# A new order of instructions and a new spread over the engines for a gated linear attention with a feed-forward layer, with the same operations and transfers

## The chip, the cores and the metric

The kernel runs on one core of a Trainium2 chip. The metric is the device time of one execution in microseconds (us). Five engines run side by side, each through a list of its own: TensorE (PE, matrix multiplications into PSUM), ScalarE (ACT), VectorE (DVE), GpSimd (POOL) and SyncE (SP). They wait for each other through semaphores. GpSimd issues the transfers of the weights, SyncE all others.

## The reference

The attention part runs over 4 batches x 8 heads, 768 steps and 48 elements a head. The feed-forward part takes the 3072 tokens of 384 elements.

```python
f = 1.0 / (1.0 + np.exp(-f_logit))
for t in range(S):
    state = f[:, :, t, :, None] * state + np.einsum('bhd,bhe->bhde', k[:, :, t], v[:, :, t])
    y[:, :, t] = np.einsum('bhd,bhde->bhe', q[:, :, t], state)
x = y.transpose(0, 2, 1, 3).reshape(B * S, H * D)
out = (np.maximum(x @ w_gate, 0.0) * (x @ w_val)) @ w_out
```

w_gate and w_val are 384 x 1536, w_out is 1536 x 384. Inputs and output are float32; the matmuls run in bfloat16.

## The kernel before

**Units.** The attention is computed in 12 units of 256 steps of one batch, in the order batch 0 to 3 for the first 256 steps, then the second, then the third. A unit loads f, k, q and v (one transfer of SyncE each, into four buffers per input). ScalarE makes exp and logarithm of f (L536, L538). PE sums the logarithms along the steps (L545, L546, "cumulative sum"). ScalarE takes exponentials of the sums (L560, L567), with which VectorE or GpSimd multiply q and k (L579, L585, written to `hats`). `hats` is transposed, by PE (L634) and a copy to `qkT`, or for later units by a transposing transfer of SyncE. PE then makes scores (L669), which are masked into `ptm`: by VectorE in one step (L683), or by a copy of ScalarE (L678) and a product of GpSimd (L680). PE forms the new state from k and v (L723, L734), VectorE and GpSimd update it (L508, L512, L515). The input v is cast into `vpad` and `vrest` by four to six small copies a unit (L380, L382 and L383 are the lines of the copy helper for VectorE's reduction form, for ScalarE, and for a plain copy). Per unit there are two y groups of PE (L767, L774, L778), of 128 steps each. A y is copied to `xT`, directly or through `xn` and a transposing transfer of SyncE (L797).

**Feed-forward.** Four y make 512 tokens. For each of 12 slices j of the hidden size, PE computes a gate group and a value group (L814, three matmuls each over xT and wg or wv), ScalarE applies relu (L819), and VectorE multiplies both into `gT` (L821). The first 512 tokens are taken in two halves of 256 for j = 0 to 2. Then, for each 128 tokens, four out groups of three matmuls (L837) sum over j; the result is copied to `osb` and stored by SyncE (L858). The weights come in four pieces of three slices for each of wg, wv, wo (288 KB each); GpSimd issues them (L477). wg0 is issued only when the second k (k1) has landed, wg3 when q3 has.

**Order.** Operations are numbered as the program adds them. Which engine an operation runs on is in a table per unit, the order on each engine in `SEQUENCE`, and which of eight PSUM banks a tile lies in, and after which other tile, in `HOMES`. The list is fixed: an engine whose next operation waits does not take one behind it. Before its first matmul of an operation PE may run `FILLERS`, matmuls of zeros whose result is not used; they stand in front of the waits for data.

```python
first = 'f0 k0 v0 q0 v1 f1 q3 q1 k1 wg0@k1 wv0@k0 wg1@f0 wv1@k0 ... wg3@q3 wo0@k0 wv3@f0 ...'.split()
FILLERS = {66: 4, 84: 11, 89: 2, 232: 5, 124: 1, 127: 2, 153: 1}
```

Some numbers that are spoken of below:

| Operation | What it is |
|---|---|
| 45, 46, 47, 48, 50, 49, 51, 53 (POOL) | issues of wg0, wv0, wg1, wv1, wv2, wg2, wg3, wv3 |
| 52, 57, 55, 56 (POOL) | issues of wo0, wo1, wo2, wo3 |
| 101, 140 (POOL) | state products of units 0 and 1 (L515) |
| 109; 281, 285 (POOL) | q products of unit 1; of unit 3 (L579) |
| 130; 254, 257, 259 (POOL) | mask products of unit 1; of unit 2 (L680) |
| 116, 245 (POOL after) | casts of v |
| 120, 122, 249, 247, 294, 292 (PE) | transposes of units 1, 2 and 3 |
| 149, 153, 145; 151, 155, 147 (PE) | gate; value groups of the first 256 tokens, j = 0 to 2 |
| 134, 137 (PE) | the two y groups of unit 1 |
| 205 to 212, 217 to 224 (PE) | out groups of the first 512 tokens; 205, 206, 217, 218 use wo0, and 211 is the first to use wo3 in the list |
| 307; 308; 309 (PE; ACT; SP) | first y group of unit 3, its copy to xn, its transposing transfer |
| 142, 270, 143, 315 (SP) | loads of k for unit 4, f for unit 5, q for unit 4, f for unit 6 |
| 369, 412 (PE) | cumulative sums of units 4 and 5 |
| 390, 435; 393 (PE; ACT) | scores of units 4 and 5; ScalarE's copy of scores of unit 4 |

Of the kernel before, what the change touches and what calls it, by code (L numbers as in the profile page):

```python
# [246 lines left out]
FILLERS = {66: 4, 84: 11, 89: 2, 232: 5, 124: 1, 127: 2, 153: 1}  # L247


def bass_hgrn2_outer__then__ffn_reglu_kernel(  # L250
# [725 lines left out]
```

## Time and profile before

| What | Value |
|---|---|
| Time, median of 3 runs | 194.19 us (193.44 to 194.41) |
| Profiled execution: its own time | 193.8 us |
| Profiled execution: span from first to last instruction | 192.0 us |
| PE busy | 181.1 us (94%) |
| DVE busy | 126.3 us (66%) |
| ACT busy | 118.5 us (62%) |
| POOL busy | 82.8 us (43%) |
| Moved by DMA | 31.89 MB, mean 166 GB/s |
| Granted TensorE clock | 1.000 |

A row of the order of events gives start, length, engine, line, operation, written and read tiles, and in brackets the idle time of the engine ahead of it and what released it. That releaser is inferred. In the chain of waits a row is start, length and what the end of the span hung on.

### The profile page before, as it was taken

How to read it: one execution, taken by the hardware profiler on the slowest of the kernel's cores; microseconds unless marked ns; L12 is line 12 of the kernel's file. 1: busy time of each engine (PE TensorE's matmuls, PEld its weight loads, DVE VectorE, ACT ScalarE, POOL GpSimd, SP SyncE). 2: the span in 40 equal slices, each digit the busy share in tenths (PEclk: the TensorE clock that was granted, in tenths of full speed). 3: DMA queues.
4: the chain of work that ended last, by engine and by line, in shares of the span. 5: the costliest groups of instructions: out<-in, count | busy, mean ns of one | idle time of the engine just before them, and what ended most of it. 6: DMA issues, size and time to landing. Idle time of an engine off the chain costs nothing.

```text
span 192.0 us, 4436 instructions
## 1 busy us (share of the span) xinstructions
PE 181.1 (94%) x1746; PEld 101.0 (53%) x1770; DVE 126.3 (66%) x238; ACT 118.5 (62%) x233; POOL 82.8 (43%) x110
## 2 busy tenths in 40 slices
PE   3998799998999999999999999999999999999994
PEld 1365474545654646455655456454655554445563
DVE  4189864879499999987669989445277452242451
ACT  4998668681997877978687857247702642433511
POOL 4458553994247256754696749007500320000000
DMA  6999999999599999999974792564144050000325
GB/s 156 324 325 285 205 253 206 242 231 199 145 310 220 229 323 255 245 213 189 259 202 79 153 232 59 120 130 123 50 107 79 0 164 3 20 0 0 81 66 164
DMA packets 79088, 31.89 MB, mean 166 GB/s; under 512 B 71254, under 2 KB 79068, under 8 KB 79068
## 3 DMA queue, kind: packets, MB, share of 16 engines
q1 hardware_dynamic: 74268, 28.08, 59.7%
q0 software_dynamic: 4800, 3.54, 11.9%
q8 instruction: 14, 0.23, 0.5%
q14 instruction: 6, 0.05, 0.1%
HBM read 25.96 MB, written 4.73 MB: 160 GB/s over the span
## 4 chain that ended last, share of the span: by engine, by line
PE 75%; DMA 6%; DVE 6%; ACT 4%; SPq 3%; issue 3%; POOL 2%; POOLq 0%
PE ps L814 43%; PE ps L837 22%; DMA wv<-in_moe_w_val_dram 4%; SPq L449 3%; DMA v_in<-in_v_dram 3%; PE ps L669 2%; PE ps L767 2%; DVE gT L821 2%; DVE ptm L683 1%; PE ps L634 1%; ACT ptm L678 1%; ACT relu L819 1%; PE ps L545 1%; DVE vpad L380 1%; POOL vpad L383 1%
## 5 line engine op out<-in xcount | busy, mean ns | idle before, releaser
L821 DVE TENSOR_TENSOR gT<-relu,ps 128x512 bf16<-128x512 bf16 (+1 forms) x75 | 47.7, 660 | 32.9 <-PE ps L814 19.6
L819 ACT ACTIVATE relu<-ps 128x512 bf16<-128x512 f32 (+1 forms) x75 | 41.8, 582 | 37.1 <-PE ps L814 29.1
L837 PE MATMUL ps<-wo,gT 128*128 128x384 bf16 (+2 forms) x300 | 56.2, 320 | 0.9 <-DVE vrest L380 0.8
L814 PE MATMUL ps<-xT,wv 128*128 128x512 bf16 (+1 forms) x214 | 54.6, 370 | 1.3 <-DMA wv<-in_moe_w_val_dram 0.4
L814 PE MATMUL ps<-xT,wg 128*128 128x512 bf16 (+1 forms) x214 | 54.2, 370 | 1.2 <-DMA wg<-in_moe_w_gate_dram 0.5
L680 POOL TENSOR_TENSOR ptm<-ptm,seen 128x512 bf16<-128x512 bf16 x21 | 24.0, 1155 | 39.9 <-ACT ptm L678 39.8
L837 PEld LDWEIGHTS ps<-wo,gT 128*128 128x128 bf16 x300 | 28.0, 98 | 22.4 <-DVE vrest L380 1.2
L814 PEld LDWEIGHTS ps<-xT,wg 128*128 128x128 bf16 x225 | 21.1, 98 | 21.3 <-DMA wg<-in_moe_w_gate_dram 0.8
L814 PEld LDWEIGHTS ps<-xT,wv 128*128 128x128 bf16 x225 | 20.9, 98 | 20.5 <-DVE hats L579 0.6
L683 DVE TENSOR_TENSOR ptm<-ps,seen 128x512 bf16<-128x512 f32 x27 | 18.1, 685 | 1.9 <-PE ps L669 1.7
L585 DVE TENSOR_TENSOR hats<-k_in,ps 64x384 bf16<-64x384 f32 x28 | 15.4, 550 | 5.2 <-ACT ps L567 4.7
L515 POOL TENSOR_TENSOR st<-ssum,dec 128x384 bf16<-128x384 f32 x16 | 13.3, 832 | 11.0 <-DVE ssum L512 10.1
L585 POOL TENSOR_TENSOR hats<-q_in,expo 64x384 bf16<-64x384 f32 x16 | 15.9, 995 | 4.8 <-ACT expo L560 3.8
L678 ACT ACTIVATE ptm<-ps 128x512 bf16<-128x512 f32 x21 | 11.8, 595 | 8.5 <-PE ps L669 8.5
L579 POOL TENSOR_TENSOR hats<-q_in,expo 128x384 bf16<-128x384 f32 x11 | 10.9, 999 | 12.8 <-ACT expo L560 8.2
L382 ACT ACTIVATE osb<-ps 128x384 f32<-128x384 f32 x13 | 6.5, 499 | 12.0 <-PE ps L837 12.0
L560 ACT ACTIVATE expo<-ps 128x384 f32<-128x384 f32 x20 | 9.4, 492 | 3.4 <-DVE ps L549 2.8
L512 DVE TENSOR_TENSOR ssum<-ps,st 128x384 f32<-128x384 f32 x16 | 8.8, 553 | 3.7 <-PE ps L723 2.3
L536 ACT ACTIVATE f_in<-f_in 128x768 f32<-128x768 f32 x12 | 10.2, 847 | 1.1 <-DMA f_in<-in_f_logit_dram 1.0
L567 ACT ACTIVATE ps<-ps 128x384 f32<-128x384 f32 x22 | 10.6, 497 | 0.0
L538 ACT ACTIVATE bneg<-f_in 128x768 bf16<-128x768 f32 x12 | 10.2, 848 | 0.2
L383 DVE COPY osb<-ps 128x384 f32<-128x384 f32 (+2 forms) x12 | 6.2, 520 | 5.5 <-PE ps L837 5.5
(86 smaller groups left out, 185.1 us busy)
## 6 DMA issues: line engine op xcount, KB each, us to landing
f_in<-in_f_logit_dram SPq DMA_DIRECT2D x12, 384.0 KB, 5.8
v_in<-in_v_dram SPq DMA_DIRECT2D x12, 384.0 KB, 5.3
q_in<-in_q_dram SPq DMA_DIRECT2D x12, 384.0 KB, 4.9
k_in<-in_k_dram SPq DMA_DIRECT2D x12, 384.0 KB, 5.4
out_dram<-osb SPq DMA_DIRECT2D x15, 192.0 KB, 2.1
out_dram<-osb SPq DMA_DIRECT2D x16, 96.0 KB, 2.2
wg<-in_moe_w_gate_dram POOLq DMA_DIRECT2D x4, 288.0 KB, 8.4
wv<-in_moe_w_val_dram POOLq DMA_DIRECT2D x4, 288.0 KB, 8.1
```

What stands on the lines that cost most here:

```text
L515: add(e, lambda: engine[e].tensor_tensor(t4(s_new), t4(tmp), rate, ALU.mult), [key] + dk, [f"S{b}_{y}"], **(dict(occ=0.79, lat=0.1) if e = ...
L536: add("ACT", lambda cut=cut: sc.activation(raw["f"][:, cut], raw["f"][:, cut], AF.Exp, scale=-1.0), [f"f{li}"], [f"f{li}"], **act_t(2 * HD ...
L567: add("ACT", lambda i=i, ex=ex: sc.activation(bc[i].ap[:, 0:HD] if in_place else ex[:, 1, :], bc[i].ap[:, 0:HD], AF.Exp, scale=1.0), [bc[i ...
L579: add(e, lambda i=i, n=n, x=x, e=e, exps=exps: engine[e].tensor_tensor(hats[:, hi, i, x, :, 0:D], by_i[n][:, i, :, :], exps(), ALU.mult), ...
L585: op = add(e, lambda i=i, n=n, x=x, e=e, y=y, lo=lo, exps=exps: engine[e].tensor_tensor(hats[64 * i:64 * i + 64, hi, y, x, :, 0:D], by_i[n ...
L678: add("ACT", lambda pt=pt, s=sj[j]: sc.activation(pt, s.ap[:, :].rearrange("p (n t) -> p n t", n=NP), AF.Copy), [sj[j]], [f"raw{mis[y]}_{j ...
L680: add("POOL", lambda pt=pt, mask=mask: gp.tensor_tensor(pt, pt, mask, ALU.mult), [f"raw{mis[y]}_{j}", "seen"], [f"raw{mis[y]}_{j}", f"ptm{ ...
L683: add("DVE", lambda pt=pt, mask=mask, s=sj[j]: ve.tensor_tensor(pt, s.ap[:, :].rearrange("p (n t) -> p n t", n=NP), mask, ALU.mult), [sj[j ...
L814: mm = te.matmul(bank.ap[:, 0:n], wt[:, kt, j * 128:(j + 1) * 128], xT[xi][:, kt, n0:n1], start=(kt == 0), stop=(kt == NK - 1))
L819: add("ACT", lambda: sc.activation(relu[ri][:, 0:n], gate.ap[:, 0:n], AF.Relu), [gate], [f"relu{ri}"], **act_t(n))
L821: add("DVE", lambda: ve.tensor_tensor(gT[gi][:, j, n0:n1], relu[ri][:, 0:n], val.ap[:, 0:n], ALU.mult), [val, f"relu{ri}"], [f"gT{gi}_{j}_ ...
L837: mm = te.matmul(bank.ap[:, 0:cut[1] - cut[0]], gT[gi][:, j, r * C:(r + 1) * C], wo[:, j, cut[0]:cut[1]], start=(j == 0), stop=(j == NJ - 1))
```

## The change

The set of operations, their sizes and the transfers are the same. Their numbers stay. Changed are the lists of all five engines, the banks, the fillers (31 in place of 26), and for some copies, casts and multiplies the engine:

| Group | before | after |
|---|---|---|
| casts of v to vpad and vrest | ACT 21, DVE 23, POOL 14 | ACT 14, DVE 17, POOL 27 |
| copies of y to xT or xn | ACT 18, DVE 6 | ACT 10, DVE 14 |
| copies of the output to osb | ACT 13, DVE 12 | ACT 10, DVE 15 |
| copies of PE's transposes to qkT | ACT 4, DVE 6 | ACT 5, DVE 5 |
| q multiplies | DVE 5, POOL 27 | DVE 6, POOL 26 |

The beginning of three of the lists, and the fillers:

```diff
     "PE": [
-        1040, 66, 67, 84, 92, 131, 104, 82, 105, 89, 94, 232, 260, 86, 98, 231, 120, 122, 133, 95, 124, 127, 153, 249, 145, 149, 151, 134, 137, 147,
-        247, 155, 157, 159, 161, 173, 167, 165, 163, 175, 251, 255, 177, 276, 169, 171, 179, 189, 187, 181, 183, 294, 185, 191, 292, 201, 203, 197,
-        296, 299, 193, 205, 199, 195, 206, 262, 207, 304, 208, 210, 209, 211, 307, 306, 218, 220, 263, 311, 266, 217, 369, 212, 219, 221, 395, 222,
-        223, 224, 321, 323, 319, 412, 337, 397, 325, 331, 327, 339, 329, 335, 341, 439, 333, 351, 345, 343, 428, 347, 430, 556, 387, 441, 353, 349,
-        435, 390, 355, 529, 359, 432, 361, 530, 357, 398, 442, 402, 446, 363, 574, 365, 472, 573, 458, 456, 474, 454, 464, 459, 470, 482, 460, 490,
...
+        1040, 66, 67, 84, 92, 82, 105, 94, 104, 131, 89, 98, 86, 231, 232, 120, 122, 260, 95, 124, 127, 249, 133, 149, 153, 145, 134, 137, 151, 155,
+        247, 165, 159, 157, 161, 147, 167, 175, 255, 251, 171, 304, 179, 169, 276, 173, 163, 177, 191, 185, 181, 189, 294, 187, 292, 193, 201, 183,
+        197, 296, 299, 199, 203, 195, 307, 218, 206, 217, 205, 207, 219, 306, 262, 209, 208, 369, 211, 221, 210, 311, 263, 266, 220, 222, 319, 327,
+        321, 223, 323, 335, 212, 412, 224, 331, 325, 333, 339, 337, 329, 395, 397, 347, 341, 343, 345, 351, 556, 439, 428, 430, 387, 441, 390, 353,
+        432, 435, 529, 359, 355, 349, 573, 363, 361, 357, 530, 442, 398, 446, 402, 365, 458, 574, 459, 460, 482, 461, 454, 490, 468, 456, 472, 464,
...
     "POOL": [
-        33, 3, 8, 9, 20, 32, 6, 31, 0, 4, 1, 7, 30, 71, 35, 21, 75, 80, 117, 115, 119, 45, 109, 46, 47, 34, 48, 130, 50, 49, 51, 53, 52, 259, 285,
-        281, 57, 101, 55, 254, 56, 257, 140, 241, 242, 289, 303, 301, 269, 382, 380, 375, 401, 417, 314, 421, 427, 541, 445, 392, 394, 438, 449, 585,
...
+        33, 20, 0, 1, 3, 4, 8, 31, 9, 32, 30, 21, 80, 6, 7, 71, 119, 117, 45, 109, 46, 48, 101, 116, 47, 130, 50, 49, 51, 35, 34, 140, 53, 257, 281,
+        285, 254, 52, 57, 259, 55, 245, 56, 287, 291, 241, 242, 301, 243, 303, 380, 383, 375, 269, 427, 314, 384, 421, 417, 423, 401, 425, 424, 426,
...
     "SP": [
-        36, 38, 39, 41, 37, 58, 40, 43, 44, 54, 60, 59, 42, 61, 62, 63, 141, 270, 142, 144, 315, 309, 143, 273, 318, 271, 272, 406, 450, 386, 385,
...
+        36, 38, 39, 41, 37, 40, 43, 58, 44, 54, 60, 59, 42, 61, 62, 63, 141, 144, 309, 142, 270, 143, 315, 273, 271, 406, 272, 450, 385, 318, 386,
...
-FILLERS = {66: 4, 84: 11, 89: 2, 232: 5, 124: 1, 127: 2, 153: 1}
+FILLERS = {66: 10, 84: 9, 82: 1, 98: 8, 124: 2, 149: 1}
```

More of the change, by code (lines that the diff above doesn't have):

```diff
@@ L240 @@
-    [
-        13, 60, 29, 67, 75, 49, 50, 83, 87, 118, 123, 125, 133, 166, 107, 110, 137, 173, 170, 152, 158, 224, 192, 218, 197, 222, 204, 265, 238, 268,
-        241, 249, 255, 278, 282, 287, 292, 303, 299, 309],
-    [
-        2, 61, 64, 40, 76, 77, 82, 51, 85, 112, 120, 99, 126, 117, 165, 136, 142, 168, 183, 180, 153, 160, 221, 187, 219, 194, 227, 231, 206, 210,
-        270, 237, 275, 276, 252, 279, 283, 290, 300, 304],
+        312, 10, 61, 29, 37, 39, 44, 80, 86, 71, 112, 95, 101, 114, 127, 177, 143, 142, 148, 180, 159, 163, 189, 194, 201, 232, 266, 212, 268, 239,
@@ new lines @@
+        243, 269, 274, 255, 260, 302, 304],
+    [
+        0, 21, 16, 19, 26, 64, 34, 83, 42, 48, 50, 51, 72, 87, 88, 90, 124, 93, 172, 115, 108, 167, 136, 139, 168, 181, 215, 196, 197, 200, 231, 267,
+        214, 235, 272, 245, 259, 278, 279, 280, 291, 300, 285, 310],
+    [
+        1, 13, 62, 20, 30, 27, 67, 43, 79, 57, 98, 102, 126, 128, 103, 165, 137, 173, 170, 184, 153, 160, 190, 217, 222, 208, 209, 207, 211, 270, 237,
+        247, 254, 277, 258, 295, 292, 297, 307],
+    [
+        3, 6, 4, 11, 65, 24, 36, 69, 40, 49, 81, 58, 94, 99, 132, 129, 134, 111, 141, 144, 171, 183, 179, 216, 225, 191, 218, 193, 195, 227, 203, 265,
+        234, 236, 256, 287, 293, 305, 299],
@@ new lines @@
+    [
+        8, 12, 15, 18, 28, 32, 41, 78, 52, 56, 73, 92, 119, 131, 117, 130, 106, 109, 138, 145, 147, 151, 175, 185, 186, 156, 188, 192, 219, 199, 229,
+        205, 263, 242, 273, 248, 257, 283, 286, 284, 294, 301],
+    [
+        2, 7, 60, 31, 76, 77, 82, 59, 118, 104, 133, 107, 122, 146, 169, 149, 182, 157, 154, 187, 261, 226, 223, 210, 240, 249, 276, 288, 296, 306,
+        308],
+    [
+        14, 63, 17, 22, 25, 33, 66, 38, 35, 46, 54, 53, 85, 74, 89, 96, 91, 97, 100, 125, 105, 166, 110, 121, 178, 174, 140, 152, 158, 162, 161, 221,
+        230, 220, 204, 198, 213, 238, 233, 241, 244, 246, 281, 303, 298, 311],
@@ L246 @@
+    [
+        9, 5, 70, 23, 68, 75, 47, 45, 55, 84, 113, 123, 120, 116, 164, 135, 150, 176, 155, 224, 262, 228, 206, 202, 264, 271, 250, 251, 275, 252, 253,
+        282, 289, 290, 309],
 ]
-FILLERS = {66: 4, 84: 11, 89: 2, 232: 5, 124: 1, 127: 2, 153: 1}
+FILLERS = {66: 10, 84: 9, 82: 1, 98: 8, 124: 2, 149: 1}
 def bass_hgrn2_outer__then__ffn_reglu_kernel(
@@ L781, in out_of @@
         x_key = [f"xT{xi}_{r}"]
-        wait = [] if y or not {0: {'kps': False, 'qps': False, 'q0': 'POOL', 'q1': 'POOL', 'even': 'PE', 'm00': 'DVE', 'm01': 'DVE', 'm10': 'DVE', 'tk': 'DVE', 'm11': 'DVE', 'r1': 'POOL', 'tq': 'ACT', 'v11': 'ACT', 'v10': 'DVE', 'r0': 'ACT', 'v01': 'ACT', 'v00': 'DVE1', 'vb': 'DVE1', 'pr': False, 'o1': 'DVE', 'vc0': 'DVE', 'x0': 'ACT', 'x1': 'ACT', 'yy': True, 'o0': 'ACT', 'vc1': 'ACT'}, 1: {'kps': True, 'r0': 'ACT', 'm01': 'DVE', 'm00': 'DVE', 'tq': 'DVE', 'v11': 'POOL', 'even': 'PE', 'tk': 'ACT', 'q1': 'DVE', 'v00': 'DVE1', 'm11': 'POOL', 'r1': 'DVE', 'm10': 'DVE', 'v01': 'POOL', 'v10': 'POOL', 'q0': 'POOL', 'qps': False, 'yy': False, 'td': False, 'vb': 'DVE', 'vc0': 'DVE', 'o0': 'DVE', 'vc1': 'DVE', 'x0': 'ACT', 'o1': 'ACT'}, 2: {'tk': 'DVE', 'v01': 'POOL', 'kps': True, 'r1': 'ACT', 'r0': 'ACT', 'even': 'PE', 'q0': 'DVE', 'v00': 'POOL', 'v10': 'ACT', 'm00': 'DVE', 'v11': 'DVE1', 'm01': 'POOL', 'm11': 'POOL', 'tq': 'DVE', 'q1': 'POOL', 'm10': 'POOL', 'qps': True, 'x0': 'ACT', 'vc1': 'ACT', 'pr': False, 'vc0': 'DVE', 'o0': 'DVE', 'x1': 'ACT', 'vb': 'POOL'}, 4: {'v10': 'DVE1', 'v01': 'POOL', 'm00': 'DVE', 'q11': 'POOL', 'q00': 'POOL', 'q01': 'POOL', 'q0': 'POOL', 'kps': True, 'even': 'DVE', 'm01': 'DVE', 'v00': 'ACT', 'm10': 'POOL', 'q10': 'POOL', 'q1': 'POOL', 'm11': 'POOL', 'v11': 'DVE1', 'qps': False, 'tq': 'DVE', 'r0': 'ACT', 'tk': 'DVE', 'r1': 'ACT', 'yy': True, 'o1': 'ACT', 'o0': 'DVE', 'x1': 'DVE', 'x0': 'DVE'}, 10: {'m00': 'POOL', 'm10': 'POOL', 'q0': 'POOL', 'kps': True, 'q10': 'POOL', 'm01': 'POOL', 'q11': 'POOL', 'q00': 'POOL', 'v11': 'ACT', 'even': 'DVE', 'v01': 'DVE1', 'v00': 'POOL', 'q01': 'POOL', 'q1': 'POOL', 'm11': 'DVE', 'v10': 'ACT', 'td': True, 'o0': 'DVE'}, 9: {'v11': 'ACT', 'v10': 'ACT', 'even': 'DVE', 'kps': True, 'q1': 'POOL', 'm10': 'DVE', 'v00': 'ACT', 'm11': 'POOL', 'q11': 'POOL', 'm00': 'DVE', 'q00': 'POOL', 'q10': 'POOL', 'q0': 'POOL', 'q01': 'POOL', 'v01': 'DVE1', 'm01': 'DVE', 'yy': False, 'x0': 'DVE', 'td': True, 'o0': 'DVE'}, 3: {'kps': True, 'm00': 'DVE', 'm11': 'POOL', 'v11': 'DVE1', 'm10': 'POOL', 'tk': 'ACT', 'v01': 'DVE1', 'r1': 'DVE1', 'tq': 'DVE', 'q1': 'POOL', 'v00': 'DVE1', 'v10': 'POOL', 'q0': 'POOL', 'r0': 'DVE1', 'm01': 'DVE', 'even': 'DVE', 'qps': False, 'vb': 'DVE1', 'x1': 'ACT', 'o1': 'DVE', 'vc1': 'ACT', 'pr': False, 'vc0': 'DVE', 'o0': 'ACT'}, 5: {'q1': 'POOL', 'm00': 'DVE', 'kps': True, 'q11': 'POOL', 'v10': 'ACT', 'v00': 'DVE1', 'even': 'DVE', 'q01': 'POOL', 'm11': 'POOL', 'q00': 'POOL', 'q0': 'POOL', 'v11': 'POOL', 'm01': 'DVE', 'q10': 'POOL', 'v01': 'ACT', 'm10': 'DVE', 'tq': 'ACT', 'r0': 'DVE1', 'tk': 'DVE', 'r1': 'DVE1', 'qps': False, 'o1': 'ACT', 'x0': 'DVE', 'o0': 'ACT', 'yy': False}, 11: {'q0': 'POOL', 'v01': 'ACT', 'q10': 'POOL', 'm00': 'DVE', 'q01': 'POOL', 'm11': 'POOL', 'q1': 'POOL', 'q00': 'POOL', 'kps': True, 'v11': 'ACT', 'm01': 'DVE', 'q11': 'POOL', 'even': 'DVE', 'v00': 'DVE1', 'm10': 'POOL', 'v10': 'DVE1', 'yy': True, 'o1': 'DVE', 'td': True}, 7: {'v10': 'POOL', 'kps': True, 'q1': 'POOL', 'v01': 'POOL', 'q11': 'POOL', 'm00': 'DVE', 'v11': 'DVE1', 'even': 'PE', 'm10': 'POOL', 'm11': 'DVE', 'm01': 'POOL', 'q10': 'POOL', 'qps': False, 'q01': 'POOL', 'q0': 'POOL', 'o0': 'DVE', 'x1': 'DVE', 'td': True, 'x0': 'ACT', 'o1': 'ACT'}, 8: {'m10': 'DVE', 'v11': 'ACT', 'q01': 'POOL', 'm01': 'POOL', 'even': 'DVE', 'q0': 'POOL', 'v10': 'ACT', 'q1': 'POOL', 'm00': 'DVE', 'kps': True, 'q11': 'POOL', 'q00': 'POOL', 'qps': False, 'v00': 'DVE1', 'q10': 'POOL', 'v01': 'ACT', 'pr': False, 'td': True, 'x0': 'DVE'}, 6: {'v10': 'DVE1', 'v01': 'DVE1', 'q10': 'DVE', 'm10': 'DVE', 'kps': True, 'q1': 'DVE', 'even': 'PE', 'q01': 'POOL', 'm00': 'POOL', 'm01': 'POOL', 'q11': 'DVE', 'q00': 'DVE', 'm11': 'POOL', 'qps': True, 'q0': 'DVE', 'pr': False, 'o0': 'DVE', 'yy': False, 'o1': 'DVE'}}.get(u, {}).get("yy") else [f"{n}{(2 * u + 1) % NM}_{j}" for j in range(2) for n in ("raw", "ptm")]
```

27 lines of the change are left out of this document (8 added, 19 removed), and 63 rows, old and new, of the table SEQUENCE.

## The prediction

> **What bounds the kernel now.** I read the page's busy shares and slices first, then busy time by stage, then the chain of waits in order of time, and last the order of events on TensorE, GpSimd, VectorE and SyncE around the few places where TensorE stands still.
>
> ```profile
> span 192.0 us, 4436 instructions
> PE 181.1 (94%) x1746; PEld 101.0 (53%) x1770; DVE 126.3 (66%) x238; ACT 118.5 (62%) x233; POOL 82.8 (43%) x110
> PE   3998799998999999999999999999999999999994
> DMA  6999999999599999999974792564144050000325
> ```
> ```profile
> 0.00:24.00 24.00, 18.02 (x232) 9.98 (x238) 16.21 (x44) 18.35 (x35) 13.63 (x34) 1.00 1.09 259
> 24.00:40.00 16.00, 15.90 (x169) 9.58 (x171) 10.06 (x21) 11.59 (x23) 10.58 (x13) 1.00 1.24 234
> 40.00:48.00 8.00, 7.00 (x81) 4.07 (x81) 7.32 (x13) 3.67 (x9) 5.06 (x8) 1.00 1.07 211
> 48.00:184.00 136.00, 134.55 (x1230) 73.48 (x1248) 90.79 (x158) 83.91 (x165) 53.49 (x58) 1.00 0.59 142
> 184.00:192.00 8.00, 5.63 (x47) 3.90 (x45) 1.96 (x5) 0.98 (x2) 0.00 (x0) 1.00 0.41 112
> ```
> TensorE is busy for 181.1 of 192.0 us. The second fence gives, per stretch, its length, then busy time of PE, PEld, DVE, ACT and POOL. From 48 to 184 us PE idles 136.00 - 134.55 = 1.45 us in all: no order of the same instructions can take more than that out of 71% of the span. PE is free for 6.0 us before 24 us (and runs fillers there besides), 1.0 us from 40 to 48, and at the tail, whose last store the change leaves last. So the change acts in the first 48 us, where the DMA slices stand at 9: weights and loads set the pace.
>
> ```profile
> 14.27 0.90 POOL wg L477
> ...
> 15.24 0.95 POOL hats L579
> 16.19 7.17 DMA wv<-in_moe_w_val_dram
> ...
> 23.49 0.49 PE ps L814 x3
> 23.98 0.73 PE ps L767 x44
> ...
> 29.17 0.55 PE ps L669 x16
> ...
> 35.34 0.45 PE ps L634 x8
> ...
> 40.77 0.49 PE ps L837 x3
> 41.26 0.66 PE ps L814 x3
> ```
> ```profile
> 14.24 0.93 POOL L477 DMA_DIRECT2D wg<-in_moe_w_gate_dram  x1 [1.07 <-DMA k_in<-in_k_dram]
> ...
> 21.45 1.15 POOL L680 TENSOR_TENSOR ptm<-ptm,seen 128x512 bf16<-128x512 bf16 x1 [2.85 <-ACT ptm L678]
> ...
> 25.68 0.78 POOL L477 DMA_DIRECT2D wo<-in_moe_w_out_dram  x1
> ...
> 32.95 1.95 POOL L579 TENSOR_TENSOR hats<-q_in,expo 128x384 bf16<-128x384 f32 x2 [1.08 <-ACT expo L560]
> 34.84 0.80 POOL L477 DMA_DIRECT2D wo<-in_moe_w_out_dram  x1
> ...
> 36.45 0.80 POOL L477 DMA_DIRECT2D wo<-in_moe_w_out_dram  x1
> ...
> 38.38 0.80 POOL L477 DMA_DIRECT2D wo<-in_moe_w_out_dram  x1
> ```
> The chain (start, length, what) says what opens the PE-bound part: GpSimd waits 1.07 us for the second k load, issues the first wg piece, multiplies one q, issues the first wv piece at 16.19; that lands 7.17 us later, at 23.36, and PE starts on it at 23.49.
>
> **Part 1: work moved ahead of the first wv piece.** The changed GpSimd list still has wg0, the q product 109 and wv0 in this order behind the same k load. SyncE issues that load ninth, as before: f2, v1 and q1 in front of it only change places. So wv0 again lands at about 23.4.
>
> ```profile
> 21.52 0.50 PE L814 MATMUL ps<-xT,wg 128*128 128x256 bf16 x3 [0.47 <-DMA wg<-in_moe_w_gate_dram]
> 21.86 0.61 PE L634 MATMUL ps<-ident,hats 128*128 128x128 bf16 x8
> 22.30 0.82 PE L814 MATMUL ps<-xT,wg 128*128 128x256 bf16 x6
> 23.49 0.49 PE L814 MATMUL ps<-xT,wv 128*128 128x256 bf16 x3 [0.37 <-DMA wv<-in_moe_w_val_dram]
> ```
> In the PE list before, the two y groups of unit 1 (operations 134 and 137, the 0.73 us of L767 at 23.98) come behind the first wv group, 151. In the changed list they stand ahead of it. Between the landing of wg0 (21.52) and of wv0 (23.36) lie 1.84 us. Three gate groups at about 0.33 (half the step of 0.65 below) take 0.98; with 0.73 that is 1.71, so both y groups fit into time that PE now waits or gives to the transposes at 21.86, which move ahead of wg0. Gain 0.73. Operation 137 needs the mask product 130. In front of it GpSimd now has wv0, wv1, a state product, a cast and wg1, where it had wv0, wg1 and wv1; it waited 2.85 us for ACT there, which covers the two additions (0.84 and 0.5 to 0.7, the length of such casts). Even at its old time it ends at 22.60, ahead of 137's turn at about 22.8. If that cover failed, the gain would shrink to 0.26, the smaller y group.
>
> VectorE takes on four v casts and one q multiply before its first k multiply. They fall into this idle time:
>
> ```profile
> 9.11 1.03 DVE L579 TENSOR_TENSOR hats<-k_in,expo 128x384 bf16<-128x384 f32 x1 [3.32 <-DMA k_in<-in_k_dram]
> ...
> 45.44 1.11 DVE L380 TENSOR_REDUCE vrest<-v_in 64x384 bf16<-64x384 f32 x2
> ```
> A cast by reduction takes 0.55 (two in 1.11), the first row's multiply about half of 1.03, so five take 2.7 of 3.32 us: nothing, by 0.6 us. The 31 fillers for 26 all lie in such waits: nothing.
>
> **Part 2: the stop at 45.6.**
>
> ```profile
> 44.15 1.62 PE L837 MATMUL ps<-wo,gT 128*128 128x384 bf16 x9
> 46.61 0.65 PE L837 MATMUL ps<-wo,gT 128*128 128x384 bf16 x3 [0.84 <-DVE vrest L380]
> ```
> ```profile
> DMA to landing us min/median/max: 7.3/7.9/13.1
> ```
> Nine matmuls at 0.49 for three take 1.47, so PE could have gone on at 45.62 and went on at 46.61: 1.0 us lost. The row names VectorE's casts, but the group (211) needs only gT, written before those casts, and the last wo piece. That piece was issued at 38.38; with the median landing of wo (the 7.9 in the last fence) it is there at 46.3. The stop belongs to the DMA.
>
> The changed PE list has more work in front of 211: out groups 217, 218 and 219 (0.49 each), y group 307 (0.2), state group 306 (0.45) and cumulative sum 369 (0.33), less out group 210 (0.49), is 1.96 us, so PE reaches it later and the whole 1.0 can go. But the wo issues move back too. Before, the first wo stood ahead of the two q products; now two mask products (254, 257) and both q products (281, 285) precede it. With the q products from about 32.5 (their scores' chain begins a little earlier) and 254 at 1.15 behind, wo0 goes out at about 35.5, ten us later than at 25.68; wo3 at about 39.6 behind another mask product and a cast.
>
> When does PE ask for wo0? From the first wv group at 23.4 the changed list has nine 256-wide groups (0.33), eighteen 512-wide (0.65, at 41.26), three transposes (0.45), four score groups (half of 0.55) and 0.8 of small ones: 2.9 + 11.7 + 1.4 + 1.1 + 0.8 = 17.9, so at 41.2. The price: wo0 took 13.1 behind a full queue; wg0, alone in GpSimd's queue but beside loads, took 7.2 (14.24 to 21.5). By 7.2 it lands at 42.7 and PE waits 1.5; by nothing lost, 0. Before 35.5 the queue should have drained, and fewer loads compete:
>
> ```profile
> 26.00 8.96 SPq L449 DMA_DIRECT2D f_in<-in_f_logit_dram  x2
> 35.05 3.58 SPq L449 DMA_DIRECT2D k_in<-in_k_dram  x1
> ...
> 48.27 1.57 SPq L797 DMA_TRANSPOSE xT<-xn  x1
> 49.89 0.56 SPq L449 DMA_DIRECT2D q_in<-in_q_dram  x1
> ```
> SyncE's transpose 309 moves ahead of k, f, q and f loads (142, 270, 143, 315) and waits for PE's 307, which in the changed list comes right before wo0 is wanted, at 41. So from about 35 to 41.5 no load is issued, where before four issues ran on slowly. I take 0.5, nearer to none than to 1.5. The loads behind start at 42 instead of 35, but q, which stood behind 309 at 49.89, comes earlier: nothing for PE, as the next f goes out at about 43 and even by the 7.2 of a weight lands at 50, while PE's sum over it (412) is due at 54 by the same group lengths.
>
> The Trainium skill ("DMA: Bandwidth & Descriptors", Anatomy of one DMA — SWDGE) gives a transfer issued by GpSimd about 2.0 us plus its bytes over 436 GB/s: for 288 KB an estimate of 2.7 us. The trace does not agree: 7.3 to 13.1 in the row above. By that rule wo0 would land at 38.2, before PE asks.
>
> **Part 3: from 48 us on.** Moved casts and copies (13 v casts more on GpSimd, eight x copies more on VectorE, 17 instructions fewer on ScalarE) lie beside PE's work. What can cost is a PSUM bank that is opened again soon after it was filled. An example: after scores 390 the changed list has one wg or wv group and one score group before 435, which reopens a bank that ScalarE copies out (393): 0.65 + 0.27 = 0.92 us, of which the copy takes 0.60.
>
> ```profile
> L678 ACT ACTIVATE ptm<-ps 128x512 bf16<-128x512 f32 x21 | 11.8, 595 | 8.5 <-PE ps L669 8.5
> L567 ACT ACTIVATE ps<-ps 128x384 f32<-128x384 f32 x22 | 10.6, 497 | 0.0
> ```
> Counting both lists with these lengths, I find 32 places with under 0.6 us to spare, against 18. Before, 1.45 us of idle stood beside 18 such places, 0.08 each at most; 14 more would be 1.1. One instruction in the reader's way costs up to 0.50 (L567), so 7 is the upper bound; more slack elsewhere could give back some of the 1.45. I take 0.25, as part of that idle belongs to plain hand-overs.
>
> **Sum.** -0.73 - 1.0 + 0.5 + 0.25 = -0.98 us. The profiled execution took 193.8 us (1.8 around its span); that gives 192.8. The median of the runs is 194.19, 0.4 above, so I forecast 193.2.
>
> **Rivals.** *wo0 in time*: with GpSimd's queue empty and no loads, nothing waits, and -0.73 - 1.0 + 0.25 = -1.48: 192.7. For it speaks the stillness of SyncE; against it that no wo or wg here landed in under 7.2. The Trainium skill's rule for such transfers leads to this time as well.
> *wo0 by the row*: a wait of 1.5 replaces the 1.0: -0.73 - 1.0 + 1.5 + 0.25 = +0.02: 194.2. For it speaks the 7.2 of wg0.
> *Head not ready*: if 130 or the early transposes are late, only 0.26 is won there: -0.51 in all, 193.7.
> *Late readers* (slower): between 50 and 140 us ScalarE reaches the short banks one instruction late, at 0.50 a time. It eats the forecast's gain at three of the 14 places and is measurably slower from five; at seven it costs 3.5 in place of 0.25: -0.98 - 0.25 + 3.5 = +2.3, 196.5. For it speaks the doubled count; against it ScalarE's 17 instructions fewer.
>
> **Numbers.** Forecast 0.35 (half either side of the line), wo0 in time 0.28, wo0 by the row 0.15, head not ready 0.04, late readers 0.18. A difference under 0.5%, 0.97 us, is about what a measurement of this kernel can't tell from none; the line is at 193.22. Faster 0.18 + 0.28 = 0.46, same 0.17 + 0.15 + 0.04 = 0.36, slower 0.18. The range runs from 191.7 (nothing lost in parts 2 and 3 and half of the 1.45 recovered: -1.73 - 0.73) to 195.5 (late readers at five places: -1.23 + 2.5).
>
> **What would show it.** Right: L767 x44 ahead of the first wv group, which still starts near 23.5; no idle of 0.8 beside L837 near 46, at most half a us at the first wo group near 41; PE idle from 48 to 184 of 1.4 to 2 us; first wo issue near 35.5. Wrong: first wv group past 24.2, over 1 us of idle at the first wo group, or PE idle over 3 us from 48 to 184.

## The result, and the profile after

The changed kernel takes 193.13 us (median of 15 runs, 192.35 to 194.36), the kernel before 193.93 us (15 runs, 193.40 to 195.32). The ratio is 0.9955, 95% interval 0.9937 to 0.9973: about 0.9 us faster, which is little but clear of the noise. The profiled execution of the changed kernel took 192.35 us, with a span of 190.6. It is the fastest of its 15, so it shows the gain at its best. Of the runs further below, five executions that ran well above the fastest of their kernel are left out of the ratios: one of after_again, at a granted clock of 0.66, two of wg0_at_q1, and one each of early_weights and early_values.

The head of the page and the busy time of three stages, as shown for the kernel before (in the second fence: length, then busy time of PE, PEld, DVE, ACT and POOL, granted clock, DMA share, GB/s). Lines in the changed kernel are numbered one lower: L813 here is L814 there.

```profile
span 190.6 us, 4474 instructions
PE 184.8 (97%) x1775; PEld 101.8 (53%) x1775; DVE 128.7 (68%) x243; ACT 112.3 (59%) x216; POOL 88.5 (46%) x122
PE   7999899999999999999999999999999999999994
DMA  6999999998999999977998685833262300030315
```
```profile
24.00:40.00 16.00, 16.00 (x138) 9.20 (x137) 10.26 (x20) 11.66 (x25) 10.77 (x16) 1.00 1.18 223
40.00:48.00 8.00, 8.00 (x85) 4.68 (x87) 6.79 (x13) 4.49 (x10) 4.61 (x7) 1.00 1.04 191
48.00:184.00 136.00, 135.60 (x1248) 73.21 (x1248) 91.51 (x159) 77.35 (x149) 58.66 (x68) 1.00 0.63 145
```

From 24 to 48 us PE no longer stands still: 24.00 of 24.00 us, where it was 22.90. In the head, in order of events (start, length, engine, line, tiles, and in brackets the idle time ahead and what ended it):

```profile
20.41 1.15 POOL L679 TENSOR_TENSOR ptm<-ptm,seen 128x512 bf16<-128x512 bf16 x1 [0.59 <-ACT ptm L677]
...
20.74 1.15 PE L813 MATMUL ps<-xT,wg 128*128 128x256 bf16 x9
21.82 0.41 PE L766 MATMUL ps<-ptm,vpad 128*32 128x128 bf16 x16
...
23.27 0.82 PE L813 MATMUL ps<-xT,wv 128*128 128x256 bf16 x6 [0.65 <-DMA wv<-in_moe_w_val_dram]
```

The y groups (L766) stand ahead of the first wv group, which begins at 23.27, and PE still waits 0.65 us for wv0. Further on, the time from issue to landing of the wo pieces (the answer on that tile), and in order of events SyncE's issues, GpSimd's issues of wo0, wo1 and (39.06) wo3, and PE at the out groups:

```profile
DMA to landing us min/median/max: 5.6/6.0/6.2
```
```profile
30.20 5.38 SPq L448 DMA_DIRECT2D v_in<-in_v_dram  x1
...
35.07 1.57 POOL L476 DMA_DIRECT2D wo<-in_moe_w_out_dram  x2
...
39.06 0.78 POOL L476 DMA_DIRECT2D wo<-in_moe_w_out_dram  x1
...
41.28 3.08 PE L836 MATMUL ps<-wo,gT 128*128 128x384 bf16 x18
...
43.02 1.27 SPq L796 DMA_TRANSPOSE xT<-xn  x1
...
46.40 1.63 PE L836 MATMUL ps<-wo,gT 128*128 128x384 bf16 x9
```

wo goes out at 35.07, PE asks for it at 41.28 and finds it there; no row has idle time in brackets, also not near 46. SyncE issues nothing between 35.6 and 43.0. Every piece lands within 6.2 us, where 7.3 was the least before. wo3 is in by 45.3 (39.06 and 6.2), and its first use, 211, is the first of the nine matmuls at 46.40. Before, PE could have begun 211 at 45.62 and the piece came at about 46.5. So PE's turn comes 0.8 us later, because more work stands in front of it, and the piece 1.2 us earlier; by these numbers the order alone would have left a wait of 0.1 to 0.2 us at the old landing.

The last wo matmuls in both, from the answers on tile wo (time of one, then the first and last start), before and after:

```profile
L837 PE MATMUL ps<-wo,gT x300: 219/326/337, 40.6 to 189.4; 128*128 128x384 bf16 x139, 128*128 128x128 bf16 x6, 128*128 128x256 bf16 x5
```
```profile
L836 PE MATMUL ps<-wo,gT x300: 219/326/337, 41.3 to 187.6; 128*128 128x384 bf16 x139, 128*128 128x128 bf16 x6, 128*128 128x256 bf16 x5
```

From these rows and the prediction's: the first wv group comes 0.22 us earlier (23.49 to 23.27), the y groups take 0.73 out of the way, the stop near 46 took 1.0; that makes 1.95. The last wo matmul starts 1.8 us earlier (189.4 to 187.6), so all the rest of the list cost 0.15. The span is 1.4 shorter: 0.4 went behind PE's last matmul, in the last copies and stores.

### The profile page after: what moved, and what is told of

It reads as the page before. It is cut to its first block, busy times and chain, and to the rows that moved or that the text cites. A ratio compares the mean times of both kernels' runs of the same rounds, so it can differ in the third digit from the quotient of the medians.

```text
span 190.6 us, 4474 instructions
## 1 busy us (share of the span) xinstructions
PE 184.8 (97%) x1775; PEld 101.8 (53%) x1775; DVE 128.7 (68%) x243; ACT 112.3 (59%) x216; POOL 88.5 (46%) x122
## 4 chain that ended last, share of the span: by engine, by line
PE 84%; DMA 6%; DVE 2%; issue 2%; SPq 2%; POOL 1%; POOLq 0%
PE ps L813 47%; PE ps L836 25%; DMA wv<-in_moe_w_val_dram 4%; PE ps L766 3%; PE ps L668 3%; DMA v_in<-in_v_dram 3%; SPq L448 2%; PE ps L633 1%; PE ps L544 1%; PE ps L545 1%; PE ps L722 1%; PE ps L777 1%; DVE gT L820 1%; PE ps L733 1%; DVE hats L584 1%
## 5 line engine op out<-in xcount | busy, mean ns | idle before, releaser
L813 PE MATMUL ps<-xT,wv 128*128 128x512 bf16 (+1 forms) x225 | 55.2, 371 | 0.7 <-DMA wv<-in_moe_w_val_dram 0.7
L813 PE MATMUL ps<-xT,wg 128*128 128x512 bf16 (+1 forms) x225 | 55.3, 371 | 0.1
L836 PE MATMUL ps<-wo,gT 128*128 128x384 bf16 (+2 forms) x300 | 54.2, 320 | 0.0
L813 PEld LDWEIGHTS ps<-xT,wv 128*128 128x128 bf16 x225 | 21.0, 98 | 22.0 <-DVE xT L382 0.8
L813 PEld LDWEIGHTS ps<-xT,wg 128*128 128x128 bf16 x225 | 21.3, 98 | 20.8 <-DVE xn L382 0.3
L682 DVE TENSOR_TENSOR ptm<-ps,seen 128x512 bf16<-128x512 f32 x27 | 17.9, 686 | 4.2 <-PE ps L668 4.0
L578 POOL TENSOR_TENSOR hats<-q_in,expo 128x384 bf16<-128x384 f32 x10 | 10.0, 1009 | 14.0 <-DMA q_in<-in_q_dram 6.9
L382 DVE COPY osb<-ps 128x384 f32<-128x384 f32 (+2 forms) x15 | 7.8, 528 | 8.8 <-PE ps L836 8.7
L381 ACT ACTIVATE osb<-ps 128x384 f32<-128x384 f32 x10 | 4.9, 488 | 12.1 <-PE ps L836 12.0
L382 POOL CAST vpad<-v_in 64x384 bf16<-64x384 f32 x21 | 10.5, 500 | 1.9 <-DMA v_in<-in_v_dram 0.8
```

The source lines that it names most:

```text
L382: return engine[e].tensor_copy(out, src)
L682: add("DVE", lambda pt=pt, mask=mask, s=sj[j]: ve.tensor_tensor(pt, s.ap[:, :].rearrange("p (n t) -> p n t", n=NP), mask, ALU.mult), [sj[j ...
L813: mm = te.matmul(bank.ap[:, 0:n], wt[:, kt, j * 128:(j + 1) * 128], xT[xi][:, kt, n0:n1], start=(kt == 0), stop=(kt == NK - 1))
L836: mm = te.matmul(bank.ap[:, 0:cut[1] - cut[0]], gT[gi][:, j, r * C:(r + 1) * C], wo[:, j, cut[0]:cut[1]], start=(j == 0), stop=(j == NJ - 1))
```

## The experiments

Theory at the start: the gain has two sources, PE work pulled ahead of the landing of wv0, and the landing of wo3, which stopped PE near 46 and now comes in time. The rivals: the stop belonged to VectorE's casts, as the row said; and the wo landings depend on GpSimd's own queue, not on the loads that SyncE holds back. Each kernel ran in 4 to 12 executions beside the kernel before, and its ratio is to that kernel.

### What stops PE near 46: four edits of the kernel before

**y_ahead**

```diff
 "PE"
-145, 149, 151, 134, 137, 147, 247
+145, 149, 134, 137, 151, 147, 247
```

> The kernel before, with one edit: the two y groups of unit 1 (134, 137) stand ahead of the first wv group 151. Theory (the stop near 46 is the landing of wo3, a fixed moment): PE is 0.7 us earlier from 24 us on, reaches group 211 at 44.9 in place of 45.6, and waits there for wo3 until 46.6 as before: idle of 1.5 to 1.7 us beside the wo matmuls near 46, time the same within 0.2 us. Rival (the stop belongs to VectorE's casts, which move along with PE): the stop stays near 0.8 to 1.0 and 0.5 to 0.7 us are gained.

Measured: 193.77 us, ratio 0.9984 (0.9963 to 1.0004). GpSimd's mask product, the weight loads of PE's y groups, the y groups and the first wv group, and the stop:

```profile
21.62 1.14 POOL L680 TENSOR_TENSOR ptm<-ptm,seen 128x512 bf16<-128x512 bf16 x1 [2.89 <-ACT ptm L678]
...
23.15 0.23 PEld L767 LDWEIGHTS ps<-ptm,vpad 128*32 128x32 bf16 x16 [0.43 <-ACT relu L819]
23.16 0.41 PE L767 MATMUL ps<-ptm,vpad 128*32 128x128 bf16 x16
...
23.89 0.83 PE L814 MATMUL ps<-xT,wv 128*128 128x256 bf16 x6
...
46.45 0.65 PE L837 MATMUL ps<-wo,gT 128*128 128x384 bf16 x3 [0.78 <-DVE vrest L380]
```

The time stays, as the theory said, but not by its numbers. The y groups begin only at 23.16 and the wv group at 23.89. It is not the mask product that holds them: it ends at 22.76, and only 137, whose turn is at about 23.4, reads it. The row of weight loads names ScalarE's relu: in `HOMES` of the kernel before, the tile of 134 follows that of gate group 145 in its bank, so 134 waits until the relu of that group has read it. The second wv group follows near 24.22 (half of the 0.66 that two take) where it was at 24.64 (23.49 and 0.33 for the first, 0.73 and small gaps for the y): 0.4 us won, not 0.7. Of that 0.1 is left when the nine wo matmuls begin (44.05 for 44.15), and group 211 again waits to about 46.5. The move alone is worth next to nothing. In the changed kernel the tile of 134 lies in another bank, behind that of transposes 249, and the y groups follow the gate groups without a stop. The move together with the new bank was not tried by itself.

**wo3_early**

```diff
 "POOL"
-281, 57, 101, 55, 254, 56, 257
+281, 57, 55, 56, 101, 254, 257
```

> The kernel before, with one edit: GpSimd issues wo1, wo2 and wo3 (57, 55, 56) one behind the other, ahead of the state product 101 and the mask product 254; wo3 then goes out near 36.5 in place of 38.4. Theory (the stop near 46 is wo3): it lands near 44.5, no idle beside the wo matmuls near 46, 0.8 to 1.0 us gained. Rival 1 (VectorE's casts): stop and time unchanged. Rival 2 (three pieces close together land later, or mask 254 comes too late for PE): wo3 still lands past 46, or a new stop of about 1 us beside the y groups of unit 2; time unchanged.

Measured: 193.64 us, ratio 0.9990 (0.9971 to 1.0009).

```profile
34.89 2.34 POOL L477 DMA_DIRECT2D wo<-in_moe_w_out_dram  x3
...
46.48 0.65 PE L837 MATMUL ps<-wo,gT 128*128 128x384 bf16 x3 [0.66 <-DMA wo<-in_moe_w_out_dram]
```
```profile
DMA to landing us min/median/max: 7.1/9.2/13.1
```

The row now names the wo transfer itself as what ended the stop. But wo3, issued at about 36.5 in place of 38.38, still lands only past 46: 0.13 us earlier. The median from issue to landing grew from 7.9 to 9.2. The pieces come in at what the transfers yield, not a fixed time behind their issue. Rival 2 holds in its first half.

**both_parts**: the two edits above in one kernel.

> The kernel before with both edits, y groups 134 and 137 ahead of 151, and wo1 to wo3 issued ahead of 101 and 254. Theory: the two gains only add up when made together: 0.7 + 0.9 = 1.6 us gained, as much as PE gained at the two places in the changed kernel, or 1.2 if wo3 at 44.5 to 44.9 is a little late. Rival (each part's gain stands by itself): the sum of the two single runs.

Measured: 193.62 us, ratio 0.9987 (0.9966 to 1.0009).

```profile
45.93 0.65 PE L837 MATMUL ps<-wo,gT 128*128 128x384 bf16 x3 [0.68 <-DMA wo<-in_moe_w_out_dram]
```

The theory of 1.2 to 1.6 us falls; nothing is gained that can be measured. The profiled execution is the fastest of the twelve (193.04), and the stop is still there, though it ends 0.68 us earlier than before. These two moves, as they stand in the list, do not carry the change's gain.

**wo3_late**

```diff
 "POOL"
-254, 56, 257, 140, 241
+254, 257, 140, 56, 241
```

> The kernel before with the issue of wo3 (56) moved behind the mask product 257 and the state product 140, so that it goes out about 2 us later, near 40.4. Theory: wo3 lands near 48.3, the stop near 46 grows by 1.5 to 2.0 us and so does the time. Rival (VectorE's casts): stop of 0.8 to 1.0 as before, time unchanged or slightly better, as 257 comes earlier.

Measured: 194.49 us, ratio 1.0029 (1.0009 to 1.0048).

```profile
40.09 0.80 POOL L477 DMA_DIRECT2D wo<-in_moe_w_out_dram  x1
...
47.36 0.66 PE L837 MATMUL ps<-wo,gT 128*128 128x384 bf16 x3 [1.65 <-DMA wo<-in_moe_w_out_dram]
```

The stop doubles from 0.84 to 1.65, is put down to wo, and the time grows by 0.6 us. That settles the first rival: wo3 stops PE, VectorE's casts only end at nearly the same moment. The kernel says the same, as 211 reads gT and wo and nothing that these casts write, and in both_parts PE goes on at 45.93 while the casts still run, until 46.02. The size is half of what was expected, as an issue 1.7 us later lands about 0.8 later.

### Why wo lands sooner in the changed kernel

**loads_first**, the changed kernel with

```diff
 "SP"
-141, 144, 309, 142, 270, 143, 315, 273
+141, 144, 142, 270, 143, 315, 309, 273
```

> The changed kernel, with one edit: on SyncE the loads 142, 270, 143 and 315 stand ahead of the transposing transfer 309 again, so that they are issued from about 35.6 us on, beside the wo pieces. Theory (the wo pieces landed in 6.0 us only because SyncE was held): issue to landing of wo goes back to 8 to 9 us, PE waits 1.5 to 2.5 us in all at the wo groups between 41 and 48, and the time is 1.0 to 2.3 us above that of the changed kernel: 194.1 to 195.4, ratio to the kernel before 1.001 to 1.008. Rival (landing is set by GpSimd's own queue): wo stays near 6 us, no wait, ratio 0.9955 as for the changed kernel.

Measured: 194.32 us, ratio 1.0036 (1.0009 to 1.0063).

```profile
DMA to landing us min/median/max: 5.1/7.1/8.2
```
```profile
47.65 1.64 PE L836 MATMUL ps<-wo,gT 128*128 128x384 bf16 x9 [0.70 <-DMA wo<-in_moe_w_out_dram]
```

With the loads beside them the wo pieces take up to 8.2 us in place of 6.2, and the stop is back, 0.70 us, at the out groups that need wo3; 1.5 to 2.5 were expected. The first out group still does not wait. The ratio lies 0.8% above that of the changed kernel (1.6 us, from two chips), more than the 0.70 explains. In the profiled execution, 0.9 us above that of the changed kernel, a further 0.36 us was lost in the head, which the edit does not touch (below).

**loads_held**, the kernel before with

```diff
 "SP"
-141, 270, 142, 144, 315, 309, 143
+141, 144, 309, 270, 142, 315, 143
```

> The kernel before, with one edit: on SyncE the loads 144 and the transposing transfer 309 stand ahead of 270, 142 and 315, so that no load is issued from about 35 us until PE has made 307, near 47. Nothing else of the change. Theory: wo lands 6 to 7 us behind its issue in place of 7.9, wo3 near 45, the stop of 0.84 us near 46 shrinks to 0.2 or less, and 0.6 to 1.0 us are gained unless the loads held back are late for PE behind 50. Rival (GpSimd's queue sets the landing): stop and time as before.

Measured: 197.46 us, ratio 1.0209 (1.0195 to 1.0223). The landing times of wo, PE's two stops with ScalarE's wait for a load, and four stretches (granted clock, DMA share and GB/s at the end of each row):

```profile
DMA to landing us min/median/max: 7.8/8.2/12.8
```
```profile
46.28 0.65 PE L837 MATMUL ps<-wo,gT 128*128 128x384 bf16 x3 [0.75 <-DVE vrest L380]
...
52.93 0.84 ACT L536 ACTIVATE f_in<-f_in 128x768 f32<-128x768 f32 x1 [3.40 <-DMA f_in<-in_f_logit_dram]
...
54.31 0.18 PE L706 MATMUL ps<-away,other 128*128 128x16 bf16 x1 [2.15 <-ACT xT L382]
```
```profile
34.00:38.00 4.00, 4.00 (x32) 2.33 (x31) 3.97 (x8) 2.46 (x4) 3.96 (x5) 1.00 1.24 221
...
44.00:46.00 2.00, 1.53 (x9) 0.58 (x7) 1.94 (x4) 0.00 (x0) 0.74 (x1) 1.00 0.19 29
...
48.00:56.00 8.00, 5.85 (x108) 3.60 (x106) 2.08 (x5) 4.56 (x9) 0.80 (x2) 0.97 0.80 213
56.00:64.00 8.00, 8.00 (x40) 3.52 (x38) 6.88 (x13) 6.28 (x14) 3.29 (x4) 0.82 1.23 306
```

The theory falls here. SyncE issues no load from 34.2 us until 49, and yet wo takes 7.8 or more and the stop stays. The row names VectorE again, but wo3, issued at 38.03, takes 8.1 us and comes at about 46.1, just ahead of 46.28. From 44 to 46 us the DMA engines are busy for only 0.19 on average and the last piece is still not in; what it waits for there stays open. The loads held back until 49 are then late, and PE stands 2.15 us: ScalarE waits 3.40 us for an f, and the copy that PE needs stands behind that f in its list. So holding SyncE is not enough. The changed kernel also issues all four wo pieces from 35 us on, when less is under way, and its loads resume at 43. Its first stretch against the 1.24 above:

```profile
34.00:38.00 4.00, 4.00 (x32) 2.28 (x31) 2.64 (x5) 3.45 (x6) 3.98 (x6) 1.00 0.98 243
```

The late start of all four wo pieces without the hold was not tried by itself in the kernel before.

### The head

**y_behind**, the changed kernel with

```diff
 "PE"
-145, 134, 137, 151, 155
+145, 151, 134, 137, 155
```

> The changed kernel with the two y groups of unit 1 (134, 137) put back behind the first wv group 151. Theory (PE only waits for wv0 there, and no later stop takes the loss up): PE idles 1.4 us ahead of 151 in place of 0.65, everything behind is 0.7 us later, ratio to the kernel before 0.9955 + 0.0037 = 0.999. Rival (a later wait, on wo0 at 41.28 or on a PSUM bank, would take it up): 0.9955 to 0.997.

Measured: 193.04 us, ratio 0.9977 (0.9964 to 0.9989); span of the profiled execution 191.4 us.

```profile
23.32 0.49 PE L813 MATMUL ps<-xT,wv 128*128 128x256 bf16 x3 [1.49 <-DMA wv<-in_moe_w_val_dram]
```

PE's idle in front of 151 grows from 0.65 to 1.49, and the span by 0.8 us: no later wait takes it up. The ratio moves by 0.22% (0.4 us), less than the 0.7 expected, but the two intervals overlap. By the profile the theory holds; by the times the 0.4 us can't be told from none.

**wg0_at_q1**, the changed kernel with

```diff
-wg0@k1
+wg0@q1
```

> The changed kernel with the issue of wg0 released by the load of q1 in place of k1, two places earlier on SyncE: about 2 us earlier on GpSimd, with wv0 and the rest of the weights behind it. Theory (the landing of wv0 sets PE's pace at 23.3): wv0 lands 1 to 2 us earlier; PE's idle of 0.65 us and the filler in front of the gate groups go, 0.6 to 1.2 us gained on the changed kernel, ratio 0.989 to 0.993. Rival (the weight then shares the engines with the loads that the first units need): k1, q2 or q3 land 1 us later, the first y groups or scores are late by as much, ratio 0.996 to 1.0.

Measured: 193.24 us, ratio 0.9977 (0.9948 to 1.0006). wg0 goes out at 12.03 in place of 14.26, but wv0 only at 15.53: the q product 109 ahead of it waits for ScalarE. Nothing is gained, as the rival says, though its reason did not show either: in the profiled execution the first y group was 1.3 us late for another cause (below), and the first wv group, at 23.81, no longer waits for wv0. So this run does not test the theory.

### The spread of the changed kernel

Its executions lie between 192.35 and 194.36, and the profiled ones differ in the head. VectorE's q product 75 (on GpSimd in the kernel before) and GpSimd's q product 71 run at the same time. First the changed kernel, then loads_first, which is the same program up to 35 us, each with its first y group, and for loads_first its first wv group:

```profile
8.15 0.56 DVE L578 TENSOR_TENSOR hats<-q_in,expo 128x384 bf16<-128x384 f32 x1
...
8.45 1.12 POOL L578 TENSOR_TENSOR hats<-q_in,expo 128x384 bf16<-128x384 f32 x1 [1.62 <-ACT expo L559]
...
14.97 0.35 PE L766 MATMUL ps<-qkT,st 128*32 128x128 bf16 x12 [0.27 <-DVE ptm L682]
```
```profile
8.10 1.00 POOL L578 TENSOR_TENSOR hats<-q_in,expo 128x384 bf16<-128x384 f32 x1 [1.30 <-ACT expo L559]
...
8.12 1.40 DVE L578 TENSOR_TENSOR hats<-q_in,expo 128x384 bf16<-128x384 f32 x1
...
16.05 0.35 PE L766 MATMUL ps<-qkT,st 128*32 128x128 bf16 x12 [0.28 <-DVE ptm L682]
...
23.63 0.61 PE L813 MATMUL ps<-xT,wv 128*128 128x256 bf16 x4
```

Where VectorE begins first, its product takes 0.56; where GpSimd was 0.02 us ahead, it takes 1.40 and ends 0.42 behind GpSimd's. The first y group then comes 1.08 us later. At the first wv group 0.36 of it is left (23.63 for 23.27): the changed kernel stands 0.65 us there for wv0, and the late execution doesn't. In wg0_at_q1 the product takes 1.39, and the wv group comes at 23.81. The Trainium skill ("SBUF — State Buffer", SBUF: two separate sides) says that VectorE, in an instruction with two inputs in SBUF, and GpSimd exclude each other from a shared port for the whole instruction, and that the first to begin has it. The trace agrees in the main: 1.40 is near the 0.98 that is left of GpSimd's product plus the 0.55 of a product alone (1.53). Four kernels tried this, and the landing of the weights:

**after_again**, unaltered, and **q_first**:

```diff
 "DVE"
-25, 81, 12, 14, 15, 19, 75, 76, 13
+25, 12, 14, 15, 19, 75, 81, 76, 13
```

> The changed kernel once more, unaltered, beside the three that follow. Its executions spread over 2 us. Theory (the spread is made in the head: VectorE's q product 75 takes 0.56 us when it begins ahead of GpSimd's q product 71, and 1.40 when GpSimd's began first): times anywhere from 192.4 to 194.4, median near 193.1, and the profile shows 0.56 with a first y group at 15.0 us, or 1.40 with one at 16.0. Rival (the spread comes from the landings of loads): the profile shows 0.5 to 0.6 for product 75 whatever the time.

> The changed kernel with one edit: on VectorE the q product 75 stands ahead of the two v casts 81 and 76, so that it can begin at the end of ScalarE's exponential near 7.6, always ahead of GpSimd's product 71 at 8.1 or later. Theory: product 75 takes 0.55 in every run, the first y group stands near 15.0, the fastest times stay near 192.4, and the median falls by 0.3 to 0.7 us below that of the unaltered kernel. Rival (landings make the spread): median and spread as for the unaltered kernel.

Measured: after_again 192.54 us, ratio 0.9937 (0.9918 to 0.9955), five executions from 192.35 to 192.83. q_first 192.32 us, ratio 0.9929 (0.9907 to 0.9952), six executions from 191.88 to 193.05. In q_first VectorE's product begins first, as meant:

```profile
7.85 0.56 DVE L578 TENSOR_TENSOR hats<-q_in,expo 128x384 bf16<-128x384 f32 x1 [0.22 <-ACT expo L559]
...
8.28 1.00 POOL L578 TENSOR_TENSOR hats<-q_in,expo 128x384 bf16<-128x384 f32 x1 [1.30 <-ACT expo L559]
```

The median falls by 0.2 us and the fastest run by 0.5, but the intervals overlap, and the unaltered kernel hardly spread this time. That two executions with the collision reach the first wv group 0.36 and 0.54 us later is in the traces; that it makes the spread of the times is not shown. No trace of after_again bears on it. In q_first the profiled execution is the slowest of its six, though its product took 0.56: there k1 let GpSimd issue wg0 only at 14.65 (14.26 in the changed kernel), and the first wv group begins at 24.03. Another part of the spread shows in the granted clock: three of the fifteen executions of the changed kernel ran at 0.991, which is 1.7 us of full speed, and they took 193.62, 193.81 and 194.36; yet one at 0.999 took 194.09. q_first is the best kernel here, by less than these runs can tell from the changed one.

**early_weights** is q_first with wg0 released by q1 and wv0 issued ahead of the q product (`45, 46, 109` for `45, 109, 46`); **early_values** moves 151 ahead of 134 and 137 besides.

> The edit of q_first, and with it wg0 released by the load of q1 and wv0 issued right behind wg0, ahead of the q product 109: wg0 out near 12, wv0 near 13 in place of 16.2. Theory (with the collision gone, the landing of wv0 is what PE waits for at 23.3): wv0 lands by 21, the idle of 0.65 in front of group 151 goes, 0.6 to 0.9 us gained on q_first. Rival (the weights take landing time from the loads of the first four units): first y group or the scores of units 2 and 3 late by 0.5 to 1.5 us, no gain or a loss.

> early_weights, and with it PE's first wv group 151 ahead of the y groups 134 and 137, which wait for GpSimd's mask product at 21.5. Theory: the wv group (0.33 to 0.65 us) fills the time in front of the y groups, up to 0.3 us gained on early_weights. Rival: the y groups were not waiting, or wv0 lands past 21.5; no gain.

Measured: 196.78 us, ratio 1.0165 (1.0131 to 1.0200), and 197.43 us, ratio 1.0170 (1.0132 to 1.0208). In early_weights:

```profile
25.13 1.02 DVE L578 TENSOR_TENSOR hats<-k_in,ps 128x384 bf16<-128x384 f32 x2 [2.70 <-DMA k_in<-in_k_dram]
...
25.75 0.96 PE L813 MATMUL ps<-xT,wv 128*128 128x256 bf16 x6 [1.88 <-DVE hats L578]
```

The rival holds, and harder than expected: the weights take the place of the loads, and VectorE waits 2.70 us for the k of unit 2. In the changed kernel that product began at 21.44:

```profile
21.44 1.01 DVE L578 TENSOR_TENSOR hats<-k_in,ps 128x384 bf16<-128x384 f32 x2
```

Holding the first weights back (wg0 behind k1, wv0 behind the q product) is worth its 0.65 us of waiting. The trace shows less of the loss than the medians: the profiled execution is the fastest of early_weights (194.62), 1.6 us above that of q_first. Of the other five, four ran at granted clocks of 0.983 to 0.991. early_values gains nothing on early_weights, and its clock fell too (last section), so whether the move alone gains can't be read from it.

## Why the prediction was right

The predicted 193.2 stands beside 193.13 measured, and the sign is right. The line for "faster" was a difference of 0.5%; 0.45% came, which fifteen executions of each could tell from none. Step by step:

- **Part 1, the y groups.** Right in place and size: they fill the wait for wv0, 0.73 us, and y_behind takes 0.84 of idle back. wv0 landed 0.2 us earlier than the 23.4 forecast. The one condition that it names, the mask product, did not bind: "Even at its old time it ends at 22.60, ahead of 137's turn" holds in y_ahead too (22.76). What it left out is the bank of 134: with the bank of before, ScalarE's relu held PE to 23.16, and 0.4 was won in place of 0.73. The change moves that tile to another bank, and so the full 0.73 came.
- **VectorE's extra work, "nothing, by 0.6 us".** Right only where VectorE's product begins first. The row behind it was `9.11 1.03 ... x1`: one product of 1.03, not two halves. By its overlap it was already a blocked one, as GpSimd multiplied then too:

```profile
8.72 1.00 POOL L579 TENSOR_TENSOR hats<-q_in,expo 128x384 bf16<-128x384 f32 x1
...
10.41 0.50 DVE L579 TENSOR_TENSOR hats<-k_in,expo 128x384 bf16<-128x384 f32 x1
```

  Alone the product takes 0.50, so the half of 1.03 met the right length by luck. The moved q product costs nothing when it begins first; when it doesn't, the first y group comes 1.08 us later and the first wv group 0.36.
- **Part 2, the stop.** Right that wo3 is the cause against what the row names (wo3_late), and right that all of it goes. Right, too, that work moved in front of 211 makes PE come later: 0.8 us. Wrong in the landing: "That piece was issued at 38.38; with the median landing of wo (the 7.9 in the last fence) it is there at 46.3" hit the moment (46.5), but wo3_early shows that the landing does not follow the issue. wo0 went out at 35.07 (35.5 forecast) and was wanted at 41.28 (41.2 forecast; 23.4 + 17.9 is 41.3). The +0.5 for its wait was not paid: all pieces took 5.6 to 6.2 us, so the rival *wo0 in time* is what happened. Its reason, the stillness of SyncE, is half confirmed: loads_first brings a stop of 0.70 back, loads_held shows that stillness alone does nothing. The Trainium skill's rule that leads to the same time ("DMA: Bandwidth & Descriptors", Anatomy of one DMA — SWDGE) gives an estimate of 2.7 us a piece. The traces do not agree: the changed kernel has 5.6 at least, and the quickest wo piece of all kept traces took 4.2 (early_values).
- **Part 3.** The late readers did not come: PE idles 0.40 us from 48 to 184. The 1.45 before can't be set against it directly, since 24 of PE's 1770 matmuls are missing in that trace. By the start of the last wo matmul, all the rest behind the first wv group cost 0.15 us more than before, where 0.25 was forecast; no run tests what makes it up.
- **The sum.** -0.98 was forecast for the profiled execution, -1.45 came (193.8 to 192.35): 0.5 for wo0 not paid, 0.2 at wv0 and 0.1 in the rest make -1.8, and 0.4 is given back at the tail. That is the rival *wo0 in time*, -1.48. Over the medians it is -0.8. That 193.2 met 193.13 is in part luck: the forecast put 0.4 between the profiled execution and the median, and 0.8 came, which makes up for most of the 0.5 for wo0 that did not come; and the base was 194.19 from three executions, 193.93 from fifteen.

## What to carry to other kernels

An issue-to-landing median is no constant when pieces queue behind one another: ask which transfers are under way, since issuing 1.9 us earlier moved a landing by 0.1. A single move cut out of a new order can be worth nothing that can be measured (0.16% and 0.10% here): the y groups needed another bank as well. Test a move both ways, done alone and undone alone. A late start in the head is not lost in full where PE waits for a landing further on: 1.08 us became 0.36. Where the head is bound by arrivals, issuing weights sooner can take time from the loads: here the medians lost 4.5 us and the profiled executions 1.6, for a wait of 0.65.
